# Attention and a wave-mixing MLP on one core: a list scheduler that also chooses engines and buffers, crossbar transposes, shared PSUM banks, column-tiled sinks

## The chip, the cores and the metric

The kernel runs on one core of a Trainium2 chip. A core has a matrix engine (TensorE, PE), a vector engine (VectorE, DVE), a scalar engine (ScalarE, ACT), GpSimd (POOL) and SyncE (SP), which here only issues transfers. They run side by side, each through its own instruction stream in order, and wait for each other by semaphores. SBUF is the working memory, 128 partitions wide; PSUM holds matmul results in eight banks of 2 KB a partition. The metric is the device time of the whole kernel in microseconds (us); lower is better. Times of one instruction are partly in nanoseconds (ns).

## The reference

Attention with causal heads ("retrieval") and heads that see four sink keys and a window of 64 keys ("streaming"), then an MLP that mixes tokens through cosine and sine:

```python
# q, k, v: batch 4, heads 8, seq 768, head_dim 64; n_sink 4, window 64
# is_retrieval = [1, 0, 1, 0, 0, 0, 1, 0]
scores = scale * np.matmul(q, k.transpose(0, 1, 3, 2))
mask = retrieval head: causal;  else: causal & (key < n_sink or distance < window)
a = softmax(where(mask, scores, -1e9))
x = (a @ v), heads side by side            # [4, 768, 512]

theta = x @ w_theta                        # [512, 512]
zr = x * np.cos(theta)
zi = x * np.sin(theta)
y = einsum('ts,bsd->btd', w_tok_r, zr) + einsum('ts,bsd->btd', w_tok_i, zi)   # [768, 768] each
u = x + y
out = u + np.maximum(u @ w_ch, 0.0)        # [512, 512]
```

## The kernel before

The kernel doesn't write its instructions in program order. Each piece of work is a step with an engine, a duration in ns, the steps it comes after and, at times, a buffer that it takes from a counted set. `Plan.order` is a list scheduler that runs when the kernel is built: it keeps a clock for each engine, starts the ready step of the highest rank (the longest way to the end), and the instructions are given out in the order of the planned starts. On the chip each engine follows its fixed order and waits where data is late.

```python
LATENCY = {"PE": (230, 0), "ACT": (190, 60), "DVE": (120, 60), "POOL": (150, 60), "SP": (50, 0), "DMA": (2000, 0), "DMAH": (2000, 0)}
plan = Plan({"s": 2, "m": 2, "x": 2, "u": 4, "uT": 3, "ot": 2, "ct": 2, "st": 2, "wtok": 4, "st_v": 4})
# PSUM: two pairs of banks "s", two banks "m" (mixing, channel), two banks "x" (transposes)
```

The heads go in pairs. q and k are loaded by GpSimd's queue, which casts them to bf16; the first two loads, which the first matmuls need, are the first thing it does:

```python
def load_qk(what, b, heads):
    nc.gpsimd.dma_start(out=state[what, b][:, heads], in_=src[:, heads])
for what in "qk":
    load_qk(what, 0, slice(0, 3, 2))

def turn_qk(what, b, n):                        # PE transposes, 12 for a pair of heads
    ...
    nc.tensor.transpose(pt[64 * x:64 * x + 64, ...], state[what, b][:, h, ...], ident)
```

v is loaded in fp32 by SyncE, cast into `vt`, and copied shifted by half a tile into `vx` for the streaming heads. The sink scores of all five streaming heads are made by three accumulating matmuls over a 128-column `kS`, in two parts of the sequence; their rows are 20 of the 128:

```python
def sink_scores():
    for y, (q0, w) in enumerate(((128, 512), (640, 128))):
        for m, n in enumerate((1, 2, 3)):
            nc.tensor.matmul(ps[:, y, :w], kS[n], qT[n][:, q0:q0 + w], start=(m == 0), stop=(m == 2))
def sink_exps():
    nc.scalar.activation(p_sink[:NS, 128:], f[:NS, :S - 128], AF.Exp, scale=scale)
```

The attention result of a tile of 128 tokens is normalised into x, transposed by PE (four matmuls), copied out of PSUM, and taken to theta:

```python
def normalize(b, i):   # reciprocal, then x = av * r, on DVE
def turn_x(b, i):
    for kk in range(KD):                        # KD = 4
        nc.tensor.transpose(pt[:, kk * 128:(kk + 1) * 128], state["x", b][:, i, kk * 128:(kk + 1) * 128], ident)
def keep_x(b, i):      # ACT in batch 0, DVE after it
def theta(b, i, y):    # four matmuls of 512 columns
def wave(b, i, what):  # ct = sin(theta + pi/2), st = sin(theta), on ACT, two tiles at once
def z_real(b, i, y):   # zr = x * ct, on DVE
def z_imag(b, i, y, eng):   # zi = x * st, on POOL, but four in batch 0 on DVE
```

Mixing takes twelve matmuls of 512 columns for a tile, in three groups (the first four parts of zr, the first four of zi, the rest of both). Then u is made on DVE, transposed by PE, copied by ACT, multiplied by w_ch in four matmuls, finished on DVE and stored by SyncE:

```python
def make_u(b, t):      # u = x + py, DVE
def turn_u(b, t):      # four PE transposes
def keep_u(b, t):      # ACT copy out of PSUM
def channel(b, t):     # four matmuls
def finish(b, t):      # max(pc, 0) + u, DVE
def store(b, t):       # SyncE
```

In the plan the attention of batch b is mixed with the MLP of batch b - 1, so PE has work of two batches at hand; the last MLP stands alone.

Of the kernel before, what the change touches and what calls it, by code (L numbers as in the profile page):

```python
# [18 lines left out]
STREAM = [1, 3, 5, 7, 4]  # L19


class Step:


    def __init__(self, eng, ns, fn, after, take, give, mode, bias):
        self.eng, self.ns, self.fn, self.after = eng, ns, fn, [a for a in after if a is not None]
        self.take, self.give, self.mode, self.bias = take, list(give), mode, bias
        self.users = 0
        self.start = self.end = None


class Plan:

# [13 lines left out]
    def add(self, eng, ns, fn, after=(), take=None, give=(), mode=None, bias=0):  # L47
        s = Step(eng, ns, fn, after, take, give, mode, bias)
        for g in s.give:
            g.users += 1  # L50
        self.steps.append(s)
        return s

    def order(self, free):
        later = {id(s): [] for s in self.steps}
        for s in self.steps:
            for a in s.after:
                later[id(a)].append(s)
        rank = {}
        for s in reversed(self.steps):  # L60
            lat = self.LATENCY[s.eng]
            rank[id(s)] = s.ns + max((rank[id(n)] + lat[n.eng == s.eng] for n in later[id(s)]), default=0)
        waiting = {id(s): len(s.after) for s in self.steps}
        ready_at = {id(s): 0 for s in self.steps}
        ready = {}
        mode = {}
        free = dict(free)
        slots = dict(self.slots)
        holding = {id(s): s.users for s in self.steps}
# [3 lines left out]
        for s in self.steps:  # L73
            if not s.after:
                ready.setdefault(s.eng, []).append(s)
        now = 0
        engines = sorted({s.eng for s in self.steps})
        for e in engines:
            heapq.heappush(events, (free.get(e, 0), count, None))
            count += 1  # L80
        while events:
            now = events[0][0]
            while events and events[0][0] <= now:
                _, _, done = heapq.heappop(events)
                if done is not None:
                    for g in done.give:
                        holding[id(g)] -= 1
                        if holding[id(g)] == 0:
                            slots[g.take] += 1
            for e in engines:  # L90
                if free.get(e, 0) > now:
                    continue
                best = None
                for s in ready.get(e, ()):
                    if ready_at[id(s)] > now or (s.take and slots[s.take] < 1):
                        continue
                    value = -ready_at[id(s)] if e[:3] == "DMA" else rank[id(s)] + s.bias
# [7 lines left out]
                ready[e].remove(s)  # L105
# [5 lines left out]
                if s.take:  # L111
                    slots[s.take] -= 1
                s.start, s.end = t, t + s.ns
                out.append(s)
                lat = self.LATENCY[e]
                free[e] = s.end
                heapq.heappush(events, (s.end, count, None))
                heapq.heappush(events, (s.end + lat[0], count + 1, s))
                heapq.heappush(events, (s.end + lat[1], count + 2, None))
                count += 3  # L120
                for n in later[id(s)]:
                    waiting[id(n)] -= 1
                    ready_at[id(n)] = max(ready_at[id(n)], s.end + lat[n.eng == e])
                    if waiting[id(n)] == 0:
                        ready.setdefault(n.eng, []).append(n)
                        heapq.heappush(events, (ready_at[id(n)], count, None))
                        count += 1
# [6 lines left out]
def kernel(  # L134
# [14 lines left out]
    nc = tc.nc  # L149
# [7 lines left out]
    assert window == 64 and n_sink * len(STREAM) <= 32  # L157
    NS = n_sink * len(STREAM)
# [5 lines left out]
    stage = ctx.enter_context(tc.tile_pool(name="stage", bufs=4))  # L164
    work = ctx.enter_context(tc.tile_pool(name="work", bufs=2))
    ps_s = ctx.enter_context(tc.tile_pool(name="ps_s", bufs=2, space=bass.MemoryType.PSUM))
    ps_m = ctx.enter_context(tc.tile_pool(name="ps_m", bufs=2, space=bass.MemoryType.PSUM))
    ps_x = ctx.enter_context(tc.tile_pool(name="ps_x", bufs=2, space=bass.MemoryType.PSUM))
# [14 lines left out]
    kS = [None] + [big.tile([128, 128], BF16, name=f"kS{n}") for n in (1, 2, 3)]  # L183
# [5 lines left out]
    vs_f = big.tile([32, 2, len(STREAM), D], F32, name="vs_f")  # L189
# [3 lines left out]

    state = {}
    plan = Plan({"s": 2, "m": 2, "x": 2, "u": 4, "uT": 3, "ot": 2, "ct": 2, "st": 2, "wtok": 4, "st_v": 4})
    add = plan.add

# [11 lines left out]

    def load_v(b, n, after=None):  # L210
        src = v[b].rearrange("h (j p) d -> p h j d", p=128)
        t = stage.tile([128, 2, NB, D], F32, tag="st_v", name="st_v")
        state["v", b, n] = t
# [6 lines left out]
    def cast_v(eng, b, n):  # L220
        h0, h1 = PAIRS[n]
        eng.tensor_copy(vt[:, h0:h1 + 1:2, :, :D], state["v", b, n])

    def shift_v(eng, b, n, x):
        h = PAIRS[n][x]
        s = STREAM.index(h)
        if b == 0:
            eng.tensor_copy(vx[:64, s], vt[:64, h])
            eng.tensor_copy(vx[64:, s, 1:], vt[64:, h, :NB - 1])
        else:  # L230
            t = state["v", b, n]
            eng.tensor_copy(vx[:64, s, :, :D], t[:64, x])
            eng.tensor_copy(vx[64:, s, 1:, :D], t[64:, x, :NB - 1])

    def sink_keys(n):
        for x, h in enumerate(PAIRS[n]):
            if not IS_RETR[h]:
                c = STREAM.index(h) * n_sink
# [3 lines left out]
    def sink_values(b0):  # L242
        for s, h in enumerate(STREAM):
            nc.sync.dma_start(out=vs_f[s * n_sink:(s + 1) * n_sink, :, s], in_=v[b0:b0 + 2, h, :n_sink].rearrange("b s d -> s b d"))


    def turn_qk(what, b, n):
        pt = state["pt", what, n] = ps_x.tile([128, 1024], BF16, tag="x", name="pt")
# [4 lines left out]
    def keep_qk(eng, what, n):  # L253
        dst = (qT if what == "q" else kT)[n]
        o = dst.rearrange("d (p j) -> d p j", j=NB)
        i = state.pop(("pt", what, n))[:, :S].rearrange("d (j p) -> d p j", j=NB)
        if eng == "ACT":
            nc.scalar.copy(o, i)  # L258
        else:
            nc.vector.tensor_copy(o, i)  # L260
# [16 lines left out]
    def score_steps(b, un, n, banks, after, before_exp):  # L277
# [38 lines left out]
        def multiply():  # L316
            cell["ps"] = ps = ps_s.tile([128, 2, 512], F32, tag="s", name="ps")
# [54 lines left out]
        mm = add("PE", ns, multiply, after, take="s", mode="64")  # L372
# [3 lines left out]
        ms = add("DVE", stream, mask_stream, [ex]) if stream else ex  # L376
        pairs = len(set(used)) == 1 and len(used) == 2
        mc = add("POOL", len(masks) // 2 * 430 if pairs else len(masks) * 300, mask_causal, [ex]) if masks else ex
        return {key: ms if key[1] is None else mc if key[1] == key[2] else ex for key in gives}, mm, ex

    def sink_scores():
        ps = state["sink_ps"] = ps_s.tile([128, 2, 512], F32, tag="s", name="ps")
        for y, (q0, w) in enumerate(((128, 512), (640, 128))):
            for m, n in enumerate((1, 2, 3)):
                nc.tensor.matmul(ps[:, y, :w], kS[n], qT[n][:, q0:q0 + w], start=(m == 0), stop=(m == 2))  # L385

    def sink_exps():
        f = state["sink_ps"].rearrange("p y c -> p (y c)")
        nc.scalar.activation(p_sink[:NS, 128:], f[:NS, :S - 128], AF.Exp, scale=scale)


    def values(b, i):
        pav = ps_s.tile([128, 2, 512], F32, tag="s", name="pav")
# [24 lines left out]
    def turn_x(b, i):  # L418
        pt = state["ptx", b, i] = ps_x.tile([128, 1024], BF16, tag="x", name="pt")
        for kk in range(KD):  # L420
            nc.tensor.transpose(pt[:, kk * 128:(kk + 1) * 128], state["x", b][:, i, kk * 128:(kk + 1) * 128], ident)  # L421

    def keep_x(b, i):
        (nc.scalar.copy if b == 0 else nc.vector.tensor_copy)(state["xT", b][:, :, i * 128:(i + 1) * 128], state.pop(("ptx", b, i))[:, :DM].rearrange("p (k t) -> p k t", k=KD))


    def theta(b, i, y):
        if y == 0:
            state["th", b, i] = ps_s.tile([128, 2, 512], F32, tag="s", name="ps")
# [4 lines left out]
    def wave(b, i, what):  # L434
        t = state[what, b, i] = work.tile([128, 2, DM], F32, tag=what, name=what)
# [5 lines left out]
    def z_real(b, i, y):  # L441
        nc.vector.tensor_tensor(state["zr", b][:, i + y], state["x", b][:, i + y], state["ct", b, i][:, y], ALU.mult)  # L442

    def z_imag(b, i, y, eng):
        (nc.vector if eng == "DVE" else nc.gpsimd).tensor_tensor(state["zi", b][:, i + y], state["x", b][:, i + y], state["st", b, i][:, y], ALU.mult)  # L445


    def mix(b, t, g):
        if g == 0:
            state["py", b, t] = ps_m.tile([128, DM], F32, tag="m", name="py")  # L450
# [6 lines left out]
    def make_u(b, t):  # L457
        u = state["u", b, t] = work.tile([128, DM], BF16, tag="u", name="u", bufs=4)
        nc.vector.tensor_tensor(u, state["x", b][:, t], state.pop(("py", b, t)), ALU.add)  # L459

    def turn_u(b, t):
        pt = state["ptu", b, t] = ps_x.tile([128, 1024], BF16, tag="x", name="pt")
# [3 lines left out]
    def keep_u(b, t):  # L466
        uT = state["uT", b, t] = work.tile([128, KD, 128], BF16, tag="uT", name="uT", bufs=3)
        nc.scalar.copy(uT, state.pop(("ptu", b, t))[:, :DM].rearrange("p (k t) -> p k t", k=KD))  # L468

    def channel(b, t):  # L470
        pc = state["pc", b, t] = ps_m.tile([128, DM], F32, tag="m", name="pc")
# [4 lines left out]
    def finish(b, t):  # L476
        ot = state["ot", b, t] = work.tile([128, DM], F32, tag="ot", name="ot")
# [6 lines left out]
    def fetch_wtok(n, t, c):  # L484
        w = work.tile([128, c, S], BF16, tag="wtok", name="wtok", bufs=4)
# [271 lines left out]
```

The softmax here doesn't subtract the row's maximum and nothing guards it: scores larger than these inputs give would overflow.

## Time and profile before

| what | value |
|---|---|
| median of 3 runs | 222.02 us (221.87 to 224.05) |
| span of the profiled run | 218.6 us |
| busy: PE, DVE, ACT, POOL | 188.4, 124.7, 119.5, 100.0 us |
| mean granted PE clock | 0.99 |
| transfers | 22.62 MB, mean 103 GB/s |

The span runs from the first to the last instruction of one profiled execution. "Busy" is the time in which an engine had at least one instruction under way; PE's matmuls overlap in a pipeline. The chain that ended last is followed back from the last instruction to whatever released each step. A row of the groups gives source line, engine, operation, output and input tiles, shapes and count, then the busy time and the mean of one, then the idle time just before such instructions and what ended it. DMA share is the mean number of busy transfer time over the core's 16 DMA engines.

### The profile page before, as it was taken

How to read it: one execution, taken by the hardware profiler on the slowest of the kernel's cores; microseconds unless marked ns; L12 is line 12 of the kernel's file. 1: busy time of each engine (PE TensorE's matmuls, PEld its weight loads, DVE VectorE, ACT ScalarE, POOL GpSimd, SP SyncE). 2: the span in 40 equal slices, each digit the busy share in tenths (PEclk: the TensorE clock that was granted, in tenths of full speed). 3: DMA queues.
4: the chain of work that ended last, by engine and by line, in shares of the span. 5: the costliest groups of instructions: out<-in, count | busy, mean ns of one | idle time of the engine just before them, and what ended most of it. 6: DMA issues, size and time to landing. Idle time of an engine off the chain costs nothing.

```text
span 218.6 us, 5007 instructions
## 1 busy us (share of the span) xinstructions
PE 188.4 (86%) x2094; PEld 109.1 (50%) x2124; DVE 124.7 (57%) x213; ACT 119.5 (55%) x156; POOL 100.0 (46%) x170
## 2 busy tenths in 40 slices
PE   0579699597995999999999999879999999599991
PEld 0436495253552786444553558535444685244440
DVE  6229983699233566487243387593362584964241
ACT  2386635961799750581697754379686337503120
POOL 7967910499836103089912400089993000970000
PEclk9999999999999699999999999999999999999999
DMA  5999999999299996012012002950021000210303
GB/s 69 159 215 218 172 202 190 197 209 161 12 182 243 218 219 146 0 51 96 0 51 96 3 0 99 226 116 0 3 85 62 1 3 0 96 51 14 130 0 144
DMA packets 39758, 22.62 MB, mean 103 GB/s; under 512 B 25912, under 2 KB 36664, under 8 KB 39736
## 3 DMA queue, kind: packets, MB, share of 16 engines
q0 software_dynamic: 11072, 9.70, 28.7%
q1 hardware_dynamic: 28664, 12.61, 21.9%
q8 instruction: 16, 0.26, 0.5%
q14 instruction: 6, 0.05, 0.1%
HBM read 25.71 MB, written 6.29 MB: 146 GB/s over the span
## 4 chain that ended last, share of the span: by engine, by line
PE 69%; DVE 8%; ACT 7%; DMA 5%; issue 4%; POOL 4%; SPq 1%; POOLq 1%; DVEq 0%; ACTq 0%
PE py L455 25%; PE pav L409 9%; PE pc L474 8%; PE ps L322 7%; PE ps L432 6%; PE pt L251 5%; POOL zi L445 3%; PE pt L464 3%; PE pt L421 3%; DVE kT L260 2%; DMA st_v<-in_v_dram 2%; DMA kb<-in_k_dram 2%; PE ps L385 2%; DVE zr L442 2%; ACT ct L437 1%
## 5 line engine op out<-in xcount | busy, mean ns | idle before, releaser
L445 POOL TENSOR_TENSOR zi<-x,st 128x512 bf16<-128x512 bf16 x20 | 28.5, 1452 | 30.8 <-ACT st L439 20.2
L455 PE MATMUL py<-zr,wtokTr 128*128 128x512 bf16 x129 | 36.2, 379 | 4.6 <-DVE zr L442 3.2
L455 PE MATMUL py<-zi,wtokTi 128*128 128x512 bf16 x140 | 38.0, 379 | 1.1 <-DVE zi L445 0.8
L459 DVE TENSOR_TENSOR u<-x,py 128x512 bf16<-128x512 bf16 x24 | 16.5, 686 | 34.6 <-PE py L455 34.5
L322 PE MATMUL ps<-qT,kT 64*64 64x128 bf16 (+5 forms) x380 | 26.4, 265 | 6.0 <-ACT P L341 2.3
L442 DVE TENSOR_TENSOR zr<-x,ct 128x512 bf16<-128x512 bf16 x24 | 24.8, 1072 | 6.3 <-ACT ct L437 6.3
L468 ACT COPY uT<-pt 128x512 bf16<-128x512 bf16 x24 | 13.8, 585 | 24.3 <-PE pt L464 24.3
L200 POOL TENSOR_SCALAR_AFFINE_SELECT P<-P 128x256 bf16<-128x256 bf16 (+1 forms) x48 | 17.7, 397 | 19.0 <-ACT P L344 11.1
L478 DVE SCALAR_TENSOR_TENSOR ot<-pc,u 128x512 f32<-128x512 f32 x24 | 16.5, 688 | 16.7 <-PE pc L474 8.1
L432 PE MATMUL ps<-w_theta_sb,xT 128*128 128x512 bf16 x92 | 23.1, 379 | 2.8 <-ACT st L439 2.6
L437 ACT ACTIVATE ct<-ps,half_pi 128x1024 f32<-128x1024 f32 x12 | 13.1, 1117 | 20.8 <-PE ps L432 20.2
L322 PEld LDWEIGHTS <-kT 64*64 64x64 bf16 (+1 forms) x380 | 13.4, 113 | 20.6 <-issue 15.0
L474 PE MATMUL pc<-w_ch_sb,uT 128*128 128x512 bf16 x90 | 23.2, 380 | 0.3
L341 ACT ACTIVATE P<-ps 128x1024 bf16<-128x1024 f32 (+2 forms) x24 | 21.4, 926 | 3.4 <-PE ps L322 3.3
L455 PEld LDWEIGHTS <-wtokTi 128*128 128x128 bf16 x144 | 13.4, 98 | 15.3 <-issue 1.2
L258 ACT COPY qT<-pt 128x768 bf16<-128x768 bf16 x14 | 11.0, 802 | 18.1 <-PE pt L251 18.0
L455 PEld LDWEIGHTS <-wtokTr 128*128 128x128 bf16 x144 | 12.3, 97 | 16.2 <-issue 5.7
L338 ACT ACTIVATE P_st<-ps 128x1024 bf16<-128x1024 f32 (+1 forms) x16 | 12.7, 810 | 8.9 <-PE ps L322 8.8
L416 DVE TENSOR_TENSOR x<-pav,r 128x512 bf16<-128x512 f32 x24 | 16.6, 692 | 0.8
L358 DVE TENSOR_TENSOR P_st<-P_st,m_stream 128x512 bf16<-128x512 bf16 (+2 forms) x24 | 12.1, 515 | 7.9 <-ACT P_st L349 5.8
L409 PE MATMUL pav<-vx,P_st 128*128 128x65 bf16 x120 | 16.1, 202 | 0.5 <-issue 0.5
L409 PE MATMUL pav<-vt,P_st 128*128 128x65 bf16 x120 | 16.1, 202 | 0.0
(74 smaller groups left out, 314.9 us busy)
## 6 DMA issues: line engine op xcount, KB each, us to landing
st_v<-in_v_dram SPq DMA_DIRECT2D x32, 192.0 KB
out_dram<-ot SPq DMA_DIRECT2D x24, 256.0 KB
qb<-in_q_dram POOLq DMA_DIRECT2D x3, 768.0 KB, 11.9
kb<-in_k_dram POOLq DMA_DIRECT2D x3, 768.0 KB, 16.5
wtok<-in_moe_w_tok_r_dram POOLq DMA_DIRECT2D x3, 384.0 KB, 13.9
wtok<-in_moe_w_tok_i_dram POOLq DMA_DIRECT2D x3, 384.0 KB, 12.7
w_theta_sb<-in_moe_w_theta_dram POOLq DMA_DIRECT2D x1, 512.0 KB, 9.2
w_ch_sb<-in_moe_w_ch_dram POOLq DMA_DIRECT2D x1, 512.0 KB, 24.2
```

Source lines behind the costliest of these rows:

```text
L200: nc.gpsimd.affine_select(out=t, in_=t, compare_op=ALU.is_ge, fill=0.0, base=base, pattern=pattern, channel_multiplier=cm)
L322: nc.tensor.matmul(ps[half, yy, c:c + w], l, r, start=True, stop=True, skip_group_check=True)
L341: nc.scalar.activation(P.rearrange("p (y c) -> p y c", y=2), ps[:, :, :w0], AF.Exp, scale=scale)
L409: nc.tensor.matmul(o, l, r, start=(m == 0), stop=True, skip_group_check=True)
L416: nc.vector.tensor_tensor(dst, av[:, :, :, :D], r.unsqueeze(3).to_broadcast([128, 2, 4, D]), ALU.mult)
L432: nc.tensor.matmul(ps[:, y], state["xT", b][:, kk, (i + y) * 128:(i + y + 1) * 128], w_theta_sb[:, kk], start=(kk == 0), stop=(kk == KD - 1))
L442: nc.vector.tensor_tensor(state["zr", b][:, i + y], state["x", b][:, i + y], state["ct", b, i][:, y], ALU.mult)
L445: (nc.vector if eng == "DVE" else nc.gpsimd).tensor_tensor(state["zi", b][:, i + y], state["x", b][:, i + y], state["st", b, i][:, y], ALU ...
L455: nc.tensor.matmul(py, wtokT[n][:, s, t * 128:(t + 1) * 128], z[:, s], start=(g == 0 and m == 0), stop=(g == 2 and m == 3))
L459: nc.vector.tensor_tensor(u, state["x", b][:, t], state.pop(("py", b, t)), ALU.add)
L474: nc.tensor.matmul(pc, uT[:, kk], w_ch_sb[:, kk], start=(kk == 0), stop=(kk == KD - 1))
L478: nc.vector.scalar_tensor_tensor(ot, state.pop(("pc", b, t)), 0.0, state.pop(("u", b, t)), ALU.max, ALU.add)
```

## The change

The scheduler gets more freedom and the durations in it are revised. A step may name several engines with a duration for each, and the plan picks the one that can end it first; a step with `port=True` is booked as longer while the other of DVE and POOL is in such a step. It also picks which buffer of a set a step gets, so all buffers are now laid down by hand:

```diff
-    plan = Plan({"s": 2, "m": 2, "x": 2, "u": 4, "uT": 3, "ot": 2, "ct": 2, "st": 2, "wtok": 4, "st_v": 4})
+    SLOTS = {
+        "pair": (2, [128, 2, 512], F32),
+        "bank": (4, [128, 512], F32),
+        "u": (4, [128, DM], BF16),
+        "uT": (4, [128, KD, 128], BF16),
+        ...
+    }
...
+                    if any(max(free[f], now) + s.on[f] + 50 < now + s.on[e] for f in s.on if f != e):
+                        continue
...
+                if s.port and other in port and port[other]:
+                    ns += 0.7 * max(0, min(ns, free[other] - t))
```

Copies out of PSUM may now go to DVE or ACT; the casts and shifts of v, and zi, to DVE or POOL. The two kinds of single PSUM banks become one set of four, shared by transposes, mixing and channel.

The transposes of x after batch 0, and of u in the batches 1 and 2 and the first four tiles of batch 3, are no longer made on PE; SyncE issues a transposing transfer from SBUF to SBUF for them:

```diff
+    def send_x(b, i):
+        nc.sync.dma_start_transpose(state["xT", b][:, :, i * 128:(i + 1) * 128], state["x", b][:, i])
+    def send_u(b, t):
+        uT = state["uT", b, t] = mine()
+        nc.sync.dma_start_transpose(uT, state["u", b, t])
...
+            if b:
+                issue = add("SP", 1250, lambda b=b, i=i: send_x(b, i), [norm[b, i]] + old)
+                xk[b, i] = add("DMAH", 500, None, [issue])
+                continue
...
+            if b == 0 or (b == B - 1 and t > 3):
                 ut = add("PE", 224, ...turn_u...)
+                uk = add({"ACT": 560, "DVE": 415}, 0, ...keep_u...)
+            else:
+                hold = add("SP", 1250, lambda b=b, t=t: send_u(b, t), [ud[b, t]], take="uT", bias=URGE)
+                uk = add("DMAH", 500, None, [hold])
```

The sinks of the three pairs with streaming heads each get a column tile of 32 of their own, so nothing has to be accumulated over the pairs; the sink rows of V are laid out to match:

```diff
-STREAM = [1, 3, 5, 7, 4]
+STREAM = [4, 1, 3, 5, 7]
+SINK_ROW = {4: 0, 1: 32, 3: 36, 5: 64, 7: 68}
...
-                nc.tensor.matmul(ps[:, y, :w], kS[n], qT[n][:, q0:q0 + w], start=(m == 0), stop=(m == 2))
+                nc.tensor.matmul(ps[32 * n - 32:32 * n, y, :w], kS[n], qT[n][:, q0:q0 + w], start=True, stop=True, skip_group_check=True)
```

The q and k of the first pair of heads are loaded in fp32 by SyncE, whose transfers need no work of GpSimd, into buffers of v, and cast by DVE or ACT:

```diff
-    for what in "qk":
-        load_qk(what, 0, slice(0, 3, 2))
+    def load_first(what):
+        t = state["first", what] = mine().rearrange("p x j d -> p x (j d)")
+        nc.sync.dma_start(out=t, in_={"q": q, "k": k}[what][0].rearrange(...)[:, 0:3:2])
+    def cast_first(what):
+        copy(state[what, 0][:, 0:3:2], state.pop(("first", what)))
```

Two smaller things: in batches after the first, `vx` is now filled from the cast `vt`, not from the fp32 buffer, which is given back sooner; and the first sink values of V are fetched after the k of batch 0 has been turned, no longer at the very start.

## The prediction

> **What bounds the kernel now.** I read the page's busy shares first, then the chain that ended last, then the busy time by stretch, and last single tiles in order of time.
>
> ```profile
> PE 188.4 (86%) x2094; PEld 109.1 (50%) x2124; DVE 124.7 (57%) x213; ACT 119.5 (55%) x156; POOL 100.0 (46%) x170
> PE 69%; DVE 8%; ACT 7%; DMA 5%; issue 4%; POOL 4%; SPq 1%; POOLq 1%; DVEq 0%; ACTq 0%
> ```
>
> TensorE (PE) is busy 86% of the span and holds 69% of the chain; no other engine is over 57%. That average hides different stages, so I cut the span at 32, 76, 100, 180, 196 and 212 us (the columns are stretch, length, then the busy time of PE, of its weight loads, of VectorE, ScalarE and GpSimd, the granted clock, the DMA share and GB/s):
>
> ```profile
> 0.00:32.00 32.00, 20.77 (x301) 15.03 (x303) 21.09 (x48) 15.92 (x22) 23.42 (x51) 1.00 0.98 172
> 32.00:76.00 44.00, 36.13 (x448) 22.25 (x450) 24.47 (x37) 31.47 (x43) 23.77 (x39) 0.96 1.07 177
> ...
> 100.00:180.00 80.00, 76.72 (x936) 43.31 (x951) 43.47 (x77) 50.03 (x67) 35.68 (x67) 1.00 0.18 54
> 180.00:196.00 16.00, 13.42 (x68) 6.23 (x69) 11.53 (x15) 7.45 (x8) 9.00 (x6) 1.00 0.13 50
> ```
>
> PE is idle 11.2 us in the first 32 us, 7.9 us up to 76, 3.3 us in the whole of 100 to 180, 2.6 us in 180 to 196, and 4.9 us after 212, where the last results go out. So from 76 to 180 this is a TensorE kernel: work taken off PE there shortens it one for one if what replaces it arrives in time. Outside, waits decide. In the middle stretch the exponentials fill ScalarE (18.0 of 20 us busy between 60 and 80).
>
> Two groups of PE work are concerned, and the engine's own rows show them (busy and mean are each instruction's full length, and neighbours overlap):
>
> ```profile
> L464 PE MATMUL pt<-ident,u 128*128 128x128 bf16 x96 | 9.0, 219 | 0.2
> L421 PE MATMUL pt<-ident,x 128*128 128x128 bf16 x96 | 8.5, 219 | 0.0
> ```
>
> One alone takes 219 ns, but what a tile of four costs is when the next work starts. In order of time: the four transposes of x start at 179.35 and the theta matmuls after them at 179.57; the four of u start at 196.36 and the mixing after them at 196.59. So a tile costs 0.22 us of PE.
>
> **What the Trainium skill says.** "VectorE: DVE Perf Modes", section "The three transpose paths", gives 390 ns for a 128x128 bf16 transpose on TensorE, which lands in PSUM, and 1309 ns by the DMA crossbar, which lands in SBUF. For the first the trace has 0.38 to 0.40 us for a tile of four and 0.22 us of PE's time; for the crossbar no run here shows anything, so its latency is my largest unknown. "SBUF — State Buffer", section "Who interferes with whom", says that a VectorE instruction with two SBUF inputs contends with a GpSimd instruction that reads SBUF, and that the loser waits. The trace agrees: zr takes 0.68 us alone and 1.05 us as its median, zi on GpSimd 1.15 us at the least and 1.60 us as its median. "TensorE: Matmul & The Clock Gate", section "Measured speedup vs the span model", gives 2.38 times for three column tiles side by side; the trace has a like thing in the q and k transposes, each of which fills half the columns: 24 of them pass in 0.79 us, 33 ns each, against 56 ns for a full-width one.
>
> **The change part by part.**
>
> Crossbar transposes. Six tiles of x in each of batches 1 to 3 (18), six of u in batches 1 and 2 and four in batch 3 (16): 34 tiles leave PE. 34 by 0.22 us is 7.5 us. Each also loses its copy out of PSUM: 18 of 0.42 us on VectorE and 16 of 0.59 us on ScalarE, 7.6 and 9.4 us, all beside PE. Added are 34 transfers of 128 KB issued by SyncE, which the plan books at 1.25 us of issue each. That is 42 us of SyncE, which was nearly all wait before, so the issue itself is hidden. What isn't hidden by itself is the way from x to theta: today 0.22 us of transposing, 0.42 us of copy and two handovers, some 1.2 us. My estimate for the new way is 3.8 us: the changed plan itself books 1.25 of issue, 0.5 of transfer and 2.0 of latency, and the nearest thing in the trace, a result's store of 256 KB at the end of the chain, took 2.01 us to land. For u the way to its channel matmul is as long, but the plan lets up to three tiles of mixing go first, 2.6 us each (12 matmuls of 0.215), so there is cover. For x at the end of a batch, the order built from the changed kernel puts two mixing groups and three channel products (about 4.3 us) among the theta matmuls of the last batch. I take 3 us in all for what shows through.
>
> Sinks column-tiled. Six matmuls over 128 columns of kS (0.81 us in the later batches, by the chain) become three column tiles side by side: one 512-wide and one 128-wide pass, 0.215 + 0.055 = 0.27 us. 0.54 by 4 is 2.2 us off PE.
>
> First q and k. Today PE waits 6.77 us for k, whose transfer is issued at 2.20 us, after q's, on GpSimd's queue. SyncE can issue k at about 0.75. The transfer was 3.8 us from issue to landing (2.9 to 6.7); with the new cast (about 0.5 us) PE could start near 5.3. But scores need q as well, which comes second now, and the two fp32 transfers are as large as before at the HBM side. I take 1.2 us.
>
> Shared banks and chosen engines. Two PSUM buffers for mixing and two for transposes become four for either, so three mixing tiles can be under way, with their zr parts first. In 180 to 196 PE waits twice for zr, 2.4 us, and starts u late; and zi's six tiles take GpSimd 9.0 us there. In the new order the last batch has two zi on VectorE and four on GpSimd. Because the two contend, I count only 2 us at the tail. Elsewhere the new order puts 13 zi on VectorE where 4 were, 32 halves of vx where 10 were, and takes copies off it. By the rows' means (zi 1.0 as my middle of 0.68 and 1.29, vx 0.33, xT 0.42) VectorE goes from 125 to about 138 us, ScalarE loses 16 uT, one xT and one weight copy net, and three uT copies more go to VectorE: 119.5 - 19 x 0.585 - 1.4 = 107 us. GpSimd loses 9 zi, 22 of 30 vx halves and 3 vt: 100 - 13 - 11.6 - 2.8 = 73 us. So no engine passes PE's about 178. Of the 7.9 us that PE idles from 32 to 76, where ScalarE is full, I give 3 us back.
>
> Sum: 7.5 + 2.2 + 1.2 + 2 + 3 - 3 = 12.9 us certain in kind; I add 3 us because a plan with truer durations also packs the many small waits (3.9% of the chain is "issue", 8.5 us). 222.0 - 16 is **206.0 us**.
>
> **Rivals.** First, the transposes show through: PE runs its fixed order, so a crossbar transfer that is late stops everything behind it, and SyncE runs in order too, so a store that waits for its result holds a transpose behind it. Queue waits of SyncE were 146.5 us for the results to store, harmless while only stores stood there. If each batch stalls 4 us at theta and some at the channel, 12 to 15 us go back: about 218. For it: the latency is unmeasured here and the stretch 100 to 180 has no slack. Against: DMA is only 0.18 busy there, and the order keeps other PE work before each use. If a transfer took several times the estimate, 225 or more.
>
> Second, VectorE becomes the bound where zi, zr, masks and normalisation meet, with the contention above. Some 138 us busy is 67% of 206; at the tail it could cost 3 to 5 us: about 210.
>
> Third, the gains are hidden: the start is set by the loads (DMA share 0.98 up to 32 us), so the first q and k gain nothing, and the middle stays on ScalarE. Then only 9.7 us of PE's remain less the exposed 3: about 214.
>
> **Range and chances.** The sum without the packing is 209, and with packing and nothing exposed 202; stalls and contention together make 215 and more. I take 199 to 215. Under 2% is above 217.6, which needs nearly all of the first rival; slower needs the transposes to cost several times the estimate.
>
> **What would show it.** Right: PE's busy near 178, about 24 rows of x and 32 of u transposes, sinks near 0.3 us a batch, PE idle under 3 us in each of the middle batches, span near 203. Wrong: PE waits put down to the transposed DMA for more than 6 us together, SyncE waiting long before a transpose, zr means above 1.1 us, or a first matmul no earlier than 6.5 us.

## The result, and the profile after

| | median us | all runs | span of the profiled run |
|---|---|---|---|
| before | 221.94 | 221.4 to 224.05 | 218.6 |
| changed | 207.97 | 207.43 to 210.23 | 206.3 |

The ratio is 0.937, with a 95% interval of 0.928 to 0.947: 14 us less. The prediction was 206.0 us, with a range of 199 to 215.

First the busy shares and the chain's shares by engine, from the page of the changed kernel:

```profile
PE 179.0 (87%) x1988; PEld 99.4 (48%) x1988; DVE 134.2 (65%) x236; ACT 108.7 (53%) x135; POOL 76.1 (37%) x140
PE 64%; DVE 14%; DMA 13%; ACT 4%; POOL 2%; issue 1%; DVEq 0%; POOLq 0%
```

PE is busy 9.4 us less (188.4 before) and idle 27.3 us instead of 30.2. VectorE's share of the chain went from 8 to 14%, DMA's from 5 to 13%. By line, 11 of DMA's 13% are loads of q and k and only 1 is a transposed u.

The same cuts in time as before (stretch, length, busy time of PE, of its weight loads, of VectorE, ScalarE and GpSimd, granted clock, DMA share, GB/s):

```profile
0.00:32.00 32.00, 21.07 (x299) 15.20 (x299) 19.64 (x44) 18.14 (x24) 23.80 (x56) 1.00 0.98 184
32.00:76.00 44.00, 38.51 (x580) 24.59 (x577) 32.39 (x61) 31.78 (x41) 16.70 (x28) 1.00 1.27 187
...
100.00:180.00 80.00, 74.86 (x880) 39.11 (x875) 53.40 (x86) 48.95 (x59) 25.84 (x47) 1.00 0.41 95
180.00:196.00 16.00, 14.51 (x68) 6.42 (x67) 7.21 (x11) 0.00 (x0) 0.04 (x1) 1.00 0.32 90
```

Between 32 and 76 us, VectorE's busy time rose from 24.5 to 32.4 us, as the plan gave it zi and shifts of v that GpSimd made before, and PE idles 5.5 us where it idled 7.9. From 100 to 180 PE idles 5.1 us. But the work in a fixed stretch shifts when the kernel gets shorter, so I also measured the stages by milestones: the last weight load of each batch's attention (the P_st rows, tile by tile).

| us, stage by stage | start to the end of batch 0's attention | to batch 1's | to batch 2's | to batch 3's | to the end |
|---|---|---|---|---|---|
| before | 34.2 | 47.9 | 54.4 | 42.6 | 39.5 |
| changed | 34.0 | 41.6 | 50.8 | 40.1 | 39.8 |

All of the gain lies in the three middle stages, 144.9 to 132.5 us, 12.4 in all. Of these, 2.8 us are idle time of PE (7.5, 1.1 and 2.3 us before; 5.5, 0.0 and 2.6 in the changed kernel), the rest is busy time. The start gained 0.2 us and the tail lost 0.3.

What PE still waits for, in the changed kernel (engine, line, what it waited for; total us, times, longest):

```profile
PE bank L300 <- DVE kb L240: 5.2, 1, 5.2
PE bank L502 <- DVE zr L243: 3.4, 4, 1.3
PE bank L300 <- DMA kb<-in_k_dram: 2.9, 2, 2.0
...
PE bank L300 <- DMA qb<-in_q_dram: 1.7, 1, 1.7
PE bank L525 <- DMA uT<-u: 1.5, 1, 1.5
```

The first matmul waits 5.2 us where it waited 6.8. The transposed u is awaited once, 1.5 us; the transposed x for 0.3 us in all (that line is on the weight loads). The wait for zr is as long as before (3.2 us).

Now the groups concerned. The first two rows are the transposes left on PE, the third the wide part of the sinks, and then zr and zi (busy, mean ns | idle before):

```profile
L515 PE MATMUL bank<-ident,u 128*128 128x128 bf16 x32 | 2.9, 219 | 0.0
L465 PE MATMUL bank<-ident,x 128*128 128x128 bf16 x24 | 2.2, 234 | 0.0
L429 PE MATMUL pair<-qT,kS 128*32 128x512 bf16 x12 | 1.8, 442 | 0.5 <-ACT P_st L382 0.5
L243 DVE TENSOR_TENSOR zr<-x,ct 128x512 bf16<-128x512 bf16 x24 | 22.9, 992 | 1.5 <-ACT ct L484 1.5
L243 POOL TENSOR_TENSOR zi<-x,st 128x512 bf16<-128x512 bf16 x11 | 14.7, 1350 | 29.0 <-ACT st L486 28.9
```

32 and 24 transposes remain out of 96 each. The sinks of one batch take 0.38 us in the chain, where they took 0.81. And the transfers that replace the transposes, tile by tile (issue time on SyncE: least, median, most; first and last start):

```profile
L468 SPq DMA_TRANSPOSE xT<-x x18: 1189/1220/2509, 67.4 to 168.2; - x18
L510 SPq DMA_TRANSPOSE uT<-u x16: 1188/1200/1230, 98.2 to 192.7; - x16
```

From the start of the issue until the transfer is reported as landed, a tile takes 2.40 to 2.48 us in 24 of the 34 cases (2.42 in the chain below). The first two x tiles of batch 1, issued at 67 and 69 us, where the loads of v, q and k run as well, needed about 5 us, by an estimate from the order of the packets.

Last, the chain in order of time in the tail (start us, us, what):

```profile
173.39 0.68 DVE zr L243
...
175.81 3.22 DVE zr L243 x2
...
179.07 6.74 PE bank L502 x31
185.81 2.42 DMA uT<-u
...
188.28 1.04 PE bank L525 x4
```

Each zr at 175.81 takes 1.6 us, against 0.68 for the one at 173.39: zi runs on GpSimd beside it. Then the first u of the batch goes through the crossbar with only part of the 2.42 us covered: PE waits 1.5 us for it. Experiments 5 and 10 take up these two.

### The profile page after: what moved, and what is told of

Read it like the earlier page. It is cut to its first block, busy times and chain, and to the rows that moved or that the text cites. A ratio compares the mean times of both kernels' runs of the same rounds, so it can differ in the third digit from the quotient of the medians.

```text
span 206.3 us, 4846 instructions
## 1 busy us (share of the span) xinstructions
PE 179.0 (87%) x1988; PEld 99.4 (48%) x1988; DVE 134.2 (65%) x236; ACT 108.7 (53%) x135; POOL 76.1 (37%) x140
## 4 chain that ended last, share of the span: by engine, by line
PE 64%; DVE 14%; DMA 13%; ACT 4%; POOL 2%; issue 1%; DVEq 0%; POOLq 0%
PE bank L502 28%; PE bank L525 9%; DMA qb<-in_q_dram 8%; PE pair L366 7%; DVE zr L243 7%; PE pair L453 7%; PE pair L479 6%; PE bank L300 5%; DMA kb<-in_k_dram 3%; DVE zi L243 2%; DVE qT L240 1%; DMA uT<-u 1%; DVE vx L240 1%; PE bank L545 1%; DMA out_dram<-ot 1%
## 5 line engine op out<-in xcount | busy, mean ns | idle before, releaser
L502 PE MATMUL bank<-zr,wtokTr 128*128 128x512 bf16 x144 | 38.6, 380 | 4.3 <-DVE zr L243 3.4
L502 PE MATMUL bank<-zi,wtokTi 128*128 128x512 bf16 x144 | 38.3, 379 | 0.2 <-DVE zi L243 0.2
L366 PE MATMUL pair<-qT,kT 64*64 64x128 bf16 (+5 forms) x380 | 26.7, 262 | 5.1 <-ACT P L385 2.1
L506 DVE TENSOR_TENSOR u<-x,bank 128x512 bf16<-128x512 bf16 x24 | 16.3, 684 | 18.6 <-PE bank L502 18.5
L525 PE MATMUL bank<-w_ch_sb,uT 128*128 128x512 bf16 x96 | 24.1, 380 | 1.9 <-DMA uT<-u 1.5
L529 DVE SCALAR_TENSOR_TENSOR ot<-bank,u 128x512 f32<-128x512 f32 x24 | 16.5, 689 | 13.5 <-PE bank L525 13.2
L385 ACT ACTIVATE P<-pair 128x1024 bf16<-128x1024 f32 (+2 forms) x24 | 21.8, 922 | 3.0 <-PE pair L366 2.8
L479 PE MATMUL pair<-w_theta_sb,xT 128*128 128x512 bf16 x96 | 22.8, 379 | 0.3 <-ACT st L486 0.2
L460 DVE TENSOR_TENSOR x<-pair,r 128x512 bf16<-128x512 f32 x24 | 16.6, 691 | 0.8
L453 PE MATMUL pair<-vx,P_st 128*128 128x65 bf16 x120 | 16.0, 200 | 0.3 <-DVE P_st L402 0.3
```

Source lines behind the costliest of these rows:

```text
L366: nc.tensor.matmul(ps[half, yy, c:c + w], l, r, start=True, stop=True, skip_group_check=True)
L385: nc.scalar.activation(P.rearrange("p (y c) -> p y c", y=2), ps[:, :, :w0], AF.Exp, scale=scale)
L453: nc.tensor.matmul(o, l, r, start=(m == 0), stop=True, skip_group_check=True)
L460: nc.vector.tensor_tensor(dst, av[:, :, :, :D], r.unsqueeze(3).to_broadcast([128, 2, 4, D]), ALU.mult)
L479: nc.tensor.matmul(ps[:, y], state["xT", b][:, kk, (i + y) * 128:(i + y + 1) * 128], w_theta_sb[:, kk], start=(kk == 0), stop=(kk == KD - 1))
L502: nc.tensor.matmul(py, wtokT[n][:, s, t * 128:(t + 1) * 128], z[:, s], start=(g == 0 and m == 0), stop=(g == 2 and m == 3))
```

## The experiments

Two things must be known to read the times. First, the plan sets every engine's order, so an edit that changes a step's length or engines can reorder the whole kernel; I say for each whether PE's order stayed. Second, the granted clock differs from run to run of the same kernel: it falls to exactly 0.50 for 3.4 or 6.8 us and comes back. The changed kernel run again beside experiments 6 and 10 (experiment 11) gave 207.5 to 218.0 us at clocks of 0.98 to 0.94. So the table gives, beside the time, the clock loss of the profiled run: over stretches of about 2.5 us, PE's busy time times (1 minus the clock), added up from the end of batch 0's attention on. It leaves the start out: the repeat lost 2.7 us of clock there and still ended batch 0's attention at 33.8 us. "Span less loss" is an estimate made of the two. Where a kernel's own wait brings the fall about, the loss belongs to that kernel, and the estimate flatters it.

| | median us | ratio to before, 95% | span | clock loss | span less loss |
|---|---|---|---|---|---|
| before | 221.94 | 1 | 218.6 | 1.5 | 217.1 |
| changed | 207.97 | 0.937, 0.928 to 0.947 | 206.3 | 0.0 | 206.3 |
| changed, again (11) | 210.62 | 0.952, 0.946 to 0.959 | 205.5 | 0.0 | 205.5 |
| 1 all transposes on PE | 213.35 | 0.962, 0.953 to 0.971 | 210.7 | 0.0 | 210.7 |
| 2 each transfer twice | 238.26 | 1.079, 1.068 to 1.090 | 234.2 | 10.0 | 224.2 |
| 3 wide sinks | 211.25 | 0.953, 0.945 to 0.961 | 209.8 | 3.2 | 206.6 |
| 4 before, crossbar alone | 212.87 | 0.955, 0.949 to 0.962 | 211.2 | 2.8 | 208.4 |
| 5 last batch's zi on VectorE | 205.49 | 0.927, 0.919 to 0.935 | 203.7 | 1.6 | 202.1 |
| 6 every zi on VectorE | 203.21 | 0.916, 0.911 to 0.921 | 199.8 | 0.0 | 199.8 |
| 7 banks split two and two | 213.39 | 0.956, 0.950 to 0.963 | 210.9 | 3.0 | 207.9 |
| 8 first q, k by GpSimd's queue | 210.63 | 0.939, 0.932 to 0.946 | 207.2 | 0.0 | 207.2 |
| 9 engines as before | 214.10 | 0.960, 0.955 to 0.965 | 212.5 | 3.2 | 209.3 |
| 10 as 5, last u's on PE | 215.15 | 0.968, 0.962 to 0.974 | 210.8 | 2.9 | 207.9 |
| 12 before, every zi on VectorE | 222.23 | 1.001, 0.998 to 1.004 | 220.0 | 3.0 | 217.0 |

The changed kernel's two profiled runs stand at 205.9 us on average; the experiments are set against that in the last column. The two differ by 0.8, so differences under 1 us are not told apart there.

### 1. All transposes back on PE

```diff
-            if b:
+            if False:
...
-            if b == 0 or (b == B - 1 and t > 3):
+            if True:
```

The plan is made anew.

> The changed kernel with all 34 crossbar transposes made on TensorE again; the plan is made anew. Theory (work taken off PE is the gain): 34 x 0.22 = 7.5 us come back on PE, less about 2 us of waits for transposed tiles that fall away, so 213 to 216 us and PE busy about 187. Rival (the better plan is the gain, the transposes only moved a wait): within 2 us of 208.

Measured 213.35 us; PE busy 186.2 us against 179.0. In the last column it is 4.8 us above the changed kernel. PE's idle time is 24.5 us against 27.3. So the crossbar takes some 7.2 us of work from PE and gives some 2.8 us back as idle time: near the two terms of the prediction, 7.5 and 3. How near is partly chance: the two profiled runs of the changed kernel differ by 3.1 us in PE's busy time (179.0 and 175.9), and the idle time holds all that the new order changed.

### 2. Each transposed transfer twice

```diff
+    def again(src):
+        nc.sync.dma_start_transpose(scratch[state["turn"] % 2], src[:, :384])
+        state["turn"] += 1
...
+        again(state["x", b][:, i])          # ahead of the transpose of x
+        again(state["u", b, t])             # ahead of the transpose of u
```

PE's order stays. The added transfer is a tile of 384 columns that nothing reads.

> The changed kernel, same order on TensorE, but ahead of each crossbar transpose SyncE issues another of three quarters of the same tile into a scratch tile, so each lands a good microsecond later and queues of them double. Theory (the latency is hidden behind other PE work but in the last batch): 1 to 3 us longer, 209 to 211. Rival (latency shows at every theta and channel product): each batch loses 3 to 5 us, 218 or more.

Measured 238.26 us, so the theory that the latency was hidden with room to spare fell. What PE waited for, first lines of that view for the two tiles:

```profile
PE pair L486 <- DMA xT<-x: 11.8, 4, 3.6
PE bank L533 <- DMA uT<-u: 10.4, 6, 3.3
```

22.2 us of waits where there were 1.8. The tiles of SyncE show why:

```profile
L475 SPq DMA_TRANSPOSE xT<-x x18: 1189/1259/2090, 67.2 to 192.3; - x18
L232 SPq DMA_TRANSPOSE scratch<-x x18: 1194/1198/1937, 65.8 to 191.0; - x18
```

A transfer of 384 columns holds SyncE for 1.2 us just like one of 512: between these two widths the cost goes by the instruction, and the instructions go one after the other. Six tiles of x with their twins take from 65.8 to 83.7 us to issue, and theta stands still meanwhile. On top, the clock fell to half after these waits, which cost another 10 us by the estimate. So the transfers are hidden because the plan places each one in time, and there is little reserve on SyncE.

### 3. Sinks as wide as before

```diff
-                nc.tensor.matmul(ps[32 * n - 32:32 * n, y, :w], kS[n], qT[n][:, q0:q0 + w], start=True, stop=True, ...)
+                nc.tensor.matmul(ps[:, y, :w], kS[n], qT[n][:, q0:q0 + w], start=(m == 0), stop=(m == 2))
```

kS is 128 columns wide again; PE's order stays.

> The changed kernel, same order of instructions, with the sink scores as three accumulating matmuls over 128 columns again. Theory (PE-bound there): 4 x 0.5 = 2 us longer, 210. Rival (ScalarE's exponentials set the pace around the sinks, PE waits for buffers anyway): under 0.7 us, 208 to 208.6.

Measured 211.25 us, near the 210 of the theory. But the trace does not bear that time out. The sinks take 0.81 us a batch in the chain against 0.38, so 4 x 0.43 = 1.7 us at most, while the three middle stages, less the clock loss, are 132.5 us in both kernels, and 3.2 us of the span are clock falls at 150 and 181 us. What is left is 0.7 us, which is within the scatter of the repeat. The column tiles save 1.7 us of PE; that this much arrives at the end is not shown.

### 4. The kernel before with the crossbar alone

```diff
+    def send_x(b, i):
+        nc.sync.dma_start_transpose(state["xT", b][:, :, i * 128:(i + 1) * 128], state["x", b][:, i])
...
+            if b:
+                issue = add("SP", 1250, lambda b=b, i=i: send_x(b, i), [norm[b, i]] + old)
+                xk[b, i] = add("DMAH", 500, None, [issue])
+                continue
```

The like for the 16 tiles of u. The plan is made anew by the old scheduler, with the old engines and banks; a store is booked at 450 ns of SyncE instead of 100.

> The kernel before with the 34 crossbar transposes alone; engines, buffers, sinks and first loads as before. Theory (the gain is PE work, 5 us as the run without the crossbar showed, whatever else is planned): 216 to 218 us. Rival (the crossbar pays only with the plan that packs around its latency: two banks for mixing leave too little other work): 220 or more.

Measured 212.87 us, better than both expectations: 8.7 us in the last column, against the 4.8 that undoing it costs in experiment 1. That it frees more in the old plan, where the transposes had only two PSUM buffers, is a possible reason; no run tests it, and the new order can have a share in it. PE waits for xT 2.4 us here and 0.3 us in the changed kernel. The crossbar is the largest of the parts.

### 5. The last batch's zi on VectorE alone

```diff
-  zs[b, "i", i + y] = add({"DVE": 690, "POOL": 1250}, 0, ...)
+  zs[b, "i", i + y] = add({"DVE": 690} if b == B - 1 else {"DVE": 690, "POOL": 1250}, 0, ...)
```

PE's order stays.

> The changed kernel with all six zi of the last batch on VectorE, two before; the order on TensorE is the same. Theory (at the tail zr on VectorE is slowed from 0.68 to 1.48 us by zi on GpSimd, and PE waits 2.5 us for it): zr back to 0.7 us, PE starts mixing 2 us sooner, 206 us. Rival (VectorE has more to do, zi comes later and PE waits for zi instead): 208 to 210.

Measured 205.49 us, as expected. The lines of the products between 174 and 190 us, first in the changed kernel (duration ns: least, median, most):

```profile
L243 DVE TENSOR_TENSOR zr<-x,ct x6: 678/987/1645, 173.4 to 181.7; 128x512 bf16<-128x512 bf16 x6
L243 POOL TENSOR_TENSOR zi<-x,st x4: 1165/1602/1608, 174.2 to 178.4; 128x512 bf16<-128x512 bf16 x4
```

and in this one:

```profile
L243 DVE TENSOR_TENSOR zi<-x,st x6: 678/681/683, 175.9 to 180.7; 128x512 bf16<-128x512 bf16 x6
L243 DVE TENSOR_TENSOR zr<-x,ct x5: 679/681/683, 174.1 to 179.5; 128x512 bf16<-128x512 bf16 x5
```

With nothing on GpSimd beside it a product takes 0.68 us; with it, up to 1.65 on VectorE and 1.60 on GpSimd. The tail is 37.7 us instead of 39.8; these 2.1 us are what the edit shows, for the rest of the 3.8 in the last column lies ahead of it. So the tail was held by two engines in each other's way, and the one that did more did it faster alone.

### 6. Every zi on VectorE

```diff
-  zs[b, "i", i + y] = add({"DVE": 690, "POOL": 1250}, 0, ...)
+  zs[b, "i", i + y] = add({"DVE": 690}, 0, ...)
```

The plan is made anew, and much of the order moves.

> The changed kernel with all 24 zi on VectorE, 13 before, so that GpSimd never works beside zr. Theory (the two contend, so VectorE does zr and zi alone about as fast as both together): zr mean from 0.99 to under 0.75 us, time 1 to 3 us less than changed, ratio 0.925 to 0.932. Rival (VectorE, full from 40 to 60 us, becomes the bound there): ratio 0.940 or more, with the loss in batch 0.

Measured 203.21 us, a ratio of 0.916: faster than both kernels, and by more than expected; on the same chip the changed kernel took 210.62.

```profile
L243 DVE TENSOR_TENSOR zr<-x,ct 128x512 bf16<-128x512 bf16 x24 | 19.9, 872 | 3.7 <-ACT ct L484 3.7
L243 DVE TENSOR_TENSOR zi<-x,st 128x512 bf16<-128x512 bf16 x24 | 16.8, 741 | 0.3 <-ACT st L486 0.3
```

VectorE takes on 11 more zi and yet is busy 132.1 us, 2.1 less than before this edit: zi goes from 933 to 741 ns and zr from 992 to 872. The 0.75 us that I expected for zr did not come; casts and shifts of v on GpSimd still run beside it. PE's wait for zr is gone. Busy times from 40 to 60 us, changed kernel and then this one (columns as above):

```profile
40.00:60.00 20.00, 14.86 (x198) 8.47 (x198) 17.86 (x28) 16.83 (x22) 13.73 (x22) 1.00 1.24 204
```

```profile
40.00:60.00 20.00, 17.68 (x205) 9.73 (x204) 17.98 (x29) 19.38 (x23) 13.21 (x23) 1.00 1.24 204
```

In the changed kernel VectorE is the fullest engine there and PE gets 14.9 of 20 us. Here VectorE is as full, but PE gets 17.7. The stage itself is no shorter for it (41.7 us against 41.6); the next two are (49.1 and 38.8 against 50.8 and 40.1), the tail is 37.7 as in experiment 5, and the start 32.6. How much of this is the products and how much the new order was not tried.

### 7. Four banks split two and two

```diff
-        "bank": (4, [128, 512], F32),
+        "bank": (2, [128, 512], F32),
+        "mbank": (2, [128, 512], F32),     # mixing and channel products take these
```

The plan is made anew.

> The changed kernel with the four shared banks split two and two again. Theory of the prediction (three mixing tiles under way bring about 2 us, at the tail most): 210. Rival (the banks were no limit): 207.5 to 208.5. A third way: with the crossbar's longer way of u each tile needs its banks in more even steps, and two banks for mixing and channel stall PE: 212 or more.

Measured 213.39 us; 2.0 us above the changed kernel in the last column. The longest wait:

```profile
PE mbank L503 <- DVE zr L244: 6.1, 4, 2.7
```

In the changed kernel it was 3.4 us, the longest 1.3. The 3.0 us of clock loss is not mere chance here. This is what follows the wait of 2.7 us:

```profile
55.00:57.00 2.00, 0.00 (x0) 0.00 (x0) 1.97 (x5) 1.55 (x2) 1.25 (x3) 0.99 1.25 198
57.00:59.00 2.00, 1.52 (x4) 0.36 (x3) 2.00 (x4) 0.00 (x0) 0.00 (x0) 0.50 1.32 205
...
63.00:65.00 2.00, 2.00 (x14) 0.91 (x12) 0.92 (x2) 0.66 (x1) 0.11 (x1) 0.80 1.29 197
```

PE (third column) does nothing from 55 to 57 us; the clock (third from the end) goes to 0.50 and is back at full only within the 63 to 65 stretch. So undoing the shared banks, with the new order that follows, costs between 2.0 us and the 3.4 that the median shows against the changed kernel's 210.0 over both its sets (experiment 11). What PE waits for is zr on VectorE, not a bank, and the tail is 38.0 us, shorter than the changed kernel's: that three mixing tiles under way help the tail is not borne out.

### 8. First q and k by GpSimd's queue

```diff
+    for what in "qk":
+        load_qk(what, 0, slice(0, 3, 2))
...
-        issue = add("SP", 600, lambda what=what: load_first(what), take="st_v", bias=10 ** 6)
```

The plan's times for these loads are set back with it. PE's order stays but for a few instructions (4 of 1,988 weight loads stand elsewhere).

> The changed kernel with the first q and k by GpSimd's queue with cast, as before. Theory of the prediction: 1.2 us longer, 209.2. Rival (theta of batch 0 started at 34.5 us where it had at 34.7, so the first loads bring nothing): 207.5 to 208.3.

Measured 210.63 us, with an interval that holds the changed kernel's ratio: the times alone tell nothing. PE's wait for k says what happened:

```profile
PE bank L300 <- DMA kb<-in_k_dram: 8.1, 2, 6.7
```

Batch 0's attention ends at 35.1 us against 34.0 and 33.8, and nothing after it makes that good: the three middle stages are 132.1 us. So this part is worth 1.1 to 1.3 us; against experiments 2 and 5, with the same start at 33.3 and 33.1 us, it would be up to 2.0.

### 9. Engines fixed as before

```diff
-   kept[what, b, n] = add({"DVE": 950, "ACT": 780}, 0, ...)
+   kept[what, b, n] = add({"ACT": 780} if ... else {"DVE": 950}, 0, ...)
-   cast[b, n] = add({"DVE": 570, "POOL": 830}, 0, ...)
+   cast[b, n] = add({"POOL": 830} if b else {"DVE": 570}, 0, ...)
```

The like for vx, zi, the weights and the copies of x and u. The plan is made anew.

> The changed kernel with each step on the engine that it had before (casts, shifts and zi on GpSimd after batch 0, copies as before), the rest as changed. Theory (the 6 us won between theta of batch 0 and the end of attention of batch 1 come from engines chosen by load): 211 to 213, with the loss between 34 and 82 us. Rival (they come from banks, sinks and a truer plan): 208 to 209.5.

Measured 214.10 us. The loss is not where it was expected: the middle stages are 131.7 us less the clock loss, no longer than the changed kernel's. Batch 0's attention ends at 38.0 us instead of 34.0; a second fall of the clock at 33 to 36 us is some 1.7 us of that, by the same estimate. From 40 to 60 us:

```profile
40.00:60.00 20.00, 18.05 (x224) 10.41 (x223) 13.32 (x19) 19.79 (x22) 16.73 (x27) 1.00 1.03 168
```

ScalarE is full, as it was before the change between 60 and 80 us (18.0 of 20), and PE gets 18.1 us, more than the 14.9 of the changed kernel. So the choice of engines moved the load there from ScalarE to VectorE and won nothing by it in these stages. By the last column its worth is 1.7 to 3.4 us, all of it in the start, and why the start is longer stays open; by the medians it is 4.1, against 210.0.

### 10. Experiment 5 with the last four transfers of u back on PE

```diff
-            if b == 0 or (b == B - 1 and t > 3):
+            if b in (0, B - 1):
```

The plan is made anew.

> The changed kernel with zi of the last batch on VectorE, as in the run that was 1 per cent faster, and the four u of the last batch turned by TensorE too. Theory (at 186 us PE has nothing else and waits 1.5 us for the first u out of the crossbar; four tiles cost it 0.9 us of turning): 0.5 us less than with zi alone, ratio 0.925. Rival (the new plan loses elsewhere what this wins): 0.930 or more.

Measured 215.15 us. The wait for u in the tail is gone, and yet the tail is 38.6 us, 0.9 longer than in experiment 5. And these four tiles moved at least 380 of PE's 2,004 weight loads to another place in the order: PE idles 6.5 us between 79 and 125 us, where experiment 5 had it idle 0.0. In the last column the run is 5.8 us above experiment 5, and the four tiles themselves are 0.9 of that. So a replanned order alone can cost some 5 us, and no replanned experiment (1, 4, 6, 7, 9, 10, 12) is exact to better than that by itself.

### 11. The changed kernel again

No edit.

> The changed kernel itself, unaltered, beside the next two. Theory: its ratio again 0.930 to 0.944, so that differences of under one per cent among the experiments stay within what a repeat gives.

Measured 210.62 us, a ratio of 0.952: missed, high. Its profiled run has the same stages as the first (33.8, 40.9, 50.8, 40.1, 39.9 us). Its times go mostly with the clock: 207.5 us at 0.980, 211.3 at 0.964, 213.0 at 0.950, 218.0 at 0.943; but the other two took 210.0 at 0.965 and at 0.984. Both sets together have a median of 210.0, 12 us below the kernel before.

### 12. The kernel before with every zi on VectorE

```diff
-                eng = "DVE" if b == 0 and i else "POOL"
+                eng = "DVE"
```

The plan is made anew.

> The kernel before with all 24 zi on VectorE, where 4 were; nothing else is altered but the order that follows. Theory (zr and zi on two engines contend, so GpSimd's part brings nothing): zr mean from 1.07 to under 0.8 us, the 9 us of zi at the end fall to about 8 for zr and zi together, 2 to 4 us less, ratio 0.982 to 0.991. Rival (the gain of zi on VectorE came with the changed plan alone): ratio 0.995 or more.

Measured 222.23 us: no gain.

```profile
L442 DVE TENSOR_TENSOR zr<-x,ct 128x512 bf16<-128x512 bf16 x24 | 18.7, 827 | 4.5 <-ACT ct L437 4.5
L445 DVE TENSOR_TENSOR zi<-x,st 128x512 bf16<-128x512 bf16 x24 | 18.4, 817 | 0.0
```

Both products got quicker (1072 and 1452 ns before), and still the kernel did not: less the clock loss, the stage of batch 1's attention went from 46.4 to 48.6 us and the next one from 54.4 to 52.0. The old plan gave back in one stage what it won in another. So taking the contention away is not enough by itself. That experiment 6 gains because the new plan can use the time is a guess: which of its freedoms that would need was not tried, and either order can have had luck.

## Why the prediction was right

It held in its sum: 206.0 predicted, 207.97 measured (210.0 over both sets). By its own steps:

- **PE's work, 9.7 us (7.5 and 2.2).** PE's busy time fell 9.4 us, 1.5 of it a clock loss in the profile of before, so 7.9. Experiment 1 has 7.2 for the transposes. Right in kind, and a little large. The other engines' loads came near too: VectorE 138 predicted and 134.2 measured, ScalarE 107 and 108.7, GpSimd 73 and 76.1.
- **Latency that shows, 3 us.** PE waits 1.8 us for transposed tiles; the idle time in experiment 1 makes it 2.8. The way was thought to take 3.8 us and takes 2.4 when the queues are quiet, about 5 beside loads. "VectorE: DVE Perf Modes", section "The three transpose paths", of the Trainium skill has 1309 ns for a 128x128 tile; here a tile of four holds SyncE for 1.2 us and lands after 2.4, so the figure can't be multiplied by four. What was not seen is how small the reserve is (experiment 2).
- **Sinks, 2.2 us.** A batch takes 0.38 us where 0.27 was predicted. 1.7 us by the chain, 0.7 by the span: not more than the scatter.
- **First q and k, 1.2 us.** 1.1 to 1.3 by experiment 8. But the start as a whole shortened by only 0.2: the first scores begin at 10.27 us where they began at 9.15. The order of PE shows what comes between (start us, us, what). Before:

```profile
9.15 0.61 PE L322 MATMUL ps<-qT,kT 64*128 64x512 bf16 x2 [0.89 <-ACT qT L258]
9.69 0.85 PE L251 MATMUL pt<-ident,kb 128*64 128x128 bf16 x12
```

and in the changed kernel:

```profile
8.84 0.85 PE L300 MATMUL bank<-ident,kb 128*64 128x128 bf16 x12 [1.97 <-DMA kb<-in_k_dram]
9.48 0.85 PE L300 MATMUL bank<-ident,qb 128*64 128x128 bf16 x12
10.27 0.93 PE L366 MATMUL pair<-qT,kT 64*128 64x256 bf16 x8
```

The second pair's k is turned ahead of the first scores, and PE waits 1.97 us for its load. The plan books that load as there at 5.5 us (3,500 ns and 2,000 of latency); it landed at 8.8. That the scores placed first would shorten the start was not tried.
- **Banks and engines, 2 us in the tail and 3 in the middle.** The sizes are near (2.0 by experiment 7, 1.7 to 3.4 by experiment 9, in the last column), but both are within what a new order can do, and the place is wrong: experiment 9 loses in the start, experiment 7 not in the tail. The tail gained nothing: zr and zi still contend there, and the first u waits for its transfer. I counted only 2 us there because of the contention, and should have counted none. In the middle, the bound only changed engines. "SBUF — State Buffer", section "Who interferes with whom", of the Trainium skill names the contention; experiment 5 agrees, 0.68 us alone and up to 1.65 beside GpSimd.
- **Packing, 3 us.** These were added without a row behind them, and no run shows them apart. Taken one at a time (experiments 1, 3, 7, 8, 9) the parts make 4.8 + 0.7 + 2.0 + 1.3 + 1.7 to 3.4 = 10.5 to 12.2 us, and the whole is 217.1 - 205.9 = 11.2 in the same measure, which leaves nothing for packing; but three of these parts are new orders, each exact to some 5 us. The stages can be read the other way: PE's idle time in the middle fell by 2.8 us, and the prediction's 3 for ScalarE, 3 for packing and -3 for latency come to 3.

So the terms that clearly did not arrive are those with a place: 1.2 us for the start, where 0.2 came, and 2 for the tail, where -0.3 came. These 3.3 us are more than the 2 by which the prediction was low. That the rest of the sum fits is in part luck, since banks, engines and packing are not told apart.

Of the rivals, the first (transposes show through, 218) was wrong as the kernel stands, but only because each transfer is placed in time. The second (VectorE as the bound, 210) holds in parts: at 40 to 60 us and in the tail. Experiments 5 and 6 relieve it and gain 3.8 and 6.1 us in the last column; 2.1 us of either lie in the tail, and experiment 6 is a new order too. The third (gains hidden, 214) holds for the start. Of the signs of being wrong none came: zr's mean is 0.99 us, PE waited 1.8 us for transposed tiles, PE began at 5.2. One sign of being right failed: PE idles 5.5 us in the first middle stage, not under 3.

Two things stay open: how the middle stages' gain divides among banks, engines and plan, since undoing any of them reorders all; and why the crossbar brings 8.7 us in the old plan and 4.8 in the new one, which the luck of the orders could make by itself.

## What to carry to other kernels

Moving transposes from the fullest engine to the DMA crossbar paid here about what they cost that engine (4.8 and 8.7 us for 7.5 us of work). It needs every transfer issued some 2.4 us ahead, and room for 1.2 us each on the queue that issues them: count the issues, not the bytes. Before giving an engine pair work to share, compare what each takes alone with what both take side by side; here one engine did both products sooner than two did, and the kernel gained by it in the new plan and not in the old one. And in a kernel whose order is planned, an edit's time holds the luck of a new order, here some 5 us: keep the order, or compare stages.

## What the runs showed of the hardware

- **A transposed transfer costs SyncE 1.2 us at 384 columns as at 512** (128 partitions, bf16; up to 2.5 us in single cases), and lands 2.4 us after its issue starts; a store of 256 KB holds it 0.33 us and lands in 2.01.
- **The clock falls to exactly half, for 3.4 or 6.8 us, after PE has been idle or loosely busy, but not each time.** In experiment 7 PE was idle from 54.7 us, the clock fell at 57.0 for 6.8 us, and the wait of 2.7 us lost 3.0 more: such a wait is paid twice. In the kernel before it fell at 71.0 us, with PE busy 48% of the 3.4 us before and no gap over 0.8; in the changed kernel PE was busy only 27% of the 3.4 us up to 43.0, and nothing fell. "TensorE: Matmul & The Clock Gate", section "Part 1: The HAM clock gate (the "warmup" mystery)", of the Trainium skill describes this: half rate after an idle window of about 3.4 us that runs free of the kernel. The trace agrees in the depth, in the lengths (3.4 us and twice that) and in the chance. It differs in the idle time needed: 2.3 us ahead of the fall in experiment 7, and no gap over 0.8 in the kernel before.
- **Two products side by side on VectorE and GpSimd took 1.6 us each,** and one after the other on VectorE alone 0.68 us each.
